# Value tiles in two buffers, loaded two tiles ahead, with joined PSUM banks for scores and values

## The chip, the cores and the metric

The kernel runs on one core of one Trainium2 chip. A core has TensorE (PE in the rows; PEld is its weight load), VectorE (DVE), ScalarE (ACT), GpSimd (POOL) and SyncE (SP), which here issues every DMA. Each engine takes its instructions in the order in which they stand in its queue and waits on semaphores for the others. The metric is the device time of one execution in microseconds.

## The reference

Attention over chunks, then two feed-forward layers, all in float32:

```python
# attention: batch 4, heads 8, sequence 768, head size 64, 8 memory slots
for c in range(nc):                     # chunks of 32 queries
    l_start = max(0, c * 32 - 16)
    r_end = min(S, c * 32 + 32 + 8)
    k_full = np.concatenate([mem_k, k[:, :, l_start:r_end]], axis=2)
    v_full = np.concatenate([mem_v, v[:, :, l_start:r_end]], axis=2)
    scores = scale * np.matmul(q_c, k_full.transpose(0, 1, 3, 2))
    a = np.exp(scores - np.max(scores, axis=-1, keepdims=True))
    a = a / (np.sum(a, axis=-1, keepdims=True) + 1e-09)
    out[:, :, c * 32:c * 32 + 32] = np.matmul(a, v_full)
...
x = out as 3072 tokens of 512           # 4 x 768 tokens, 8 heads x 64
h = x @ w_in;  x = (h * tanh(softplus(h))) @ w_out            # 512 -> 2048 -> 512
xn = x / rms(x) * rms_g
out = (silu(xn @ w_gate) * (xn @ w_val)) @ w_out2             # 512 -> 1536 -> 512
```

## The kernel before

The 3072 tokens are 24 tiles of 128 (`TSUB`), six to a batch (`SPB`). Three tiles make a block of 384 tokens, two blocks a pair (`TPP` = 6 tiles), and there are four pairs. Attention makes a pair's tokens; the first feed-forward product of that pair then runs beside the attention of the next pair.

Attention of a tile is five steps on TensorE, each with a step behind it on the other engines: `a` transposes queries and keys (L349, L306), `b` multiplies them into scores, 64 small matmuls over two PSUM banks (L371), `c` transposes the exponentials (L404), `d` multiplies them with the values, again 64 matmuls over two banks (L422), `e` transposes the result (L450). `b1` takes the maximum (L385) and subtracts it (L386) bank by bank and takes the exponential; `d1` divides by the sum (L436 to L440), also bank by bank. The steps of successive tiles are staggered by `att_list`: in one round stand `e` of tile t-4, `d` of t-3, `c` of t-2, `b` of t-1 and `a` of t. All of them take PSUM banks from `bank()`, which rotates through three.

Keys, queries and values come by `load_k`, `load_q`, `load_v`. The values go to one buffer, `vw`: two halves of eight heads, four overlapping chunks each, so eight DMAs a tile, with two more for the memory slots in the first tile of a batch. `mem_v_copy` then copies the memory values to the other three chunks on VectorE (L296), two copies a batch. A tile's values are loaded once the value product of the tile before has been issued.

The products are computed by a scheme with seven products of half size in place of eight. Six matmuls (L526 to L528, twice) are one product, seven products one group (`group`, `group1`), and a group has four banks X, Y, Z, V. X, Y and Z take a second product each, so a bank's first result must be read before the second is added, and its last result before the next group writes it. The reads are L537, L545 and L589 on ScalarE and L541, L553, L556 and L558 on VectorE. `group_banks(5)` hands the banks out in turn from five. Before a pair's first group, its tokens are added up (L502, L503 on VectorE, L504, L505 on GpSimd) and split into a high and a low part (`split`, L136 on ScalarE, L137 on VectorE) for seven operands `T`. The first of these needs the first block alone, the others both.

The weights are loaded raw (L132), converted (`cv_all`, L166 to L219) and kept or stored. The conversions are spread over the stages in small steps (`cv_upto`).

The order on each engine is not that of the code: a scheduler places the instructions by its own estimate of when each is ready. So an edit of banks, buffers or loads moves instructions on all engines.

## Time and profile before

| what | us |
|---|---|
| median of three runs | 1248.97 (1245.0 to 1252.62) |
| the profiled execution | 1247.89, of which its span 1246.1 |
| TensorE busy in the span | 1189.9 |
| VectorE busy | 858.1 |
| ScalarE busy | 623.7 |
| GpSimd busy | 289.0 |
| fill: attention of the first pair | 0 to 82 |
| first product beside attention, three stages | 82 to 181.5, 268.7, 358.5 |
| first product without attention | 358.5 to 422.4 |
| the rest | 422.4 to 1246 |

The profile is one execution. A matmul's busy time holds its way through the array, so successive matmuls overlap, and a busy TensorE is not one at its peak; the distance between starts tells the pace. The granted clock of TensorE is told as a share of full speed: 1.00 is 2.4 GHz, 0.50 is 1.2 GHz.

### The profile page before, as it was taken

What the parts mean: (1) busy time and instruction counts of PE and PEld (TensorE: products, weight loads), DVE (VectorE), ACT (ScalarE), POOL (GpSimd) and SP (SyncE); (2) the same over time, 40 slices, a digit from 0 to 9 for tenths busy, and PEclk for the clock granted to TensorE, in tenths of its full rate; (3) what the DMA queues carried; (4) which work ended last, traced back from release to release, by engine and by line L of the source; (5) the groups of instructions that cost most, each with busy time, mean ns of one, the idle gap of its engine ahead of it and who ended that gap; (6) DMA issues with size and microseconds to landing.
All of it is one profiled execution on the core that took longest, in us unless ns stands there. A gap on an engine that the chain in (4) does not pass through costs nothing.

```text
span 1246.1 us, 24931 instructions
## 1 busy us (share of the span) xinstructions
PE 1189.9 (95%) x9896; PEld 1144.8 (92%) x9896; DVE 858.1 (69%) x1418; ACT 623.7 (50%) x1050; POOL 289.0 (23%) x233
## 2 busy tenths in 40 slices
PE   5979899989979899999999999999999999999998
PEld 4768799979979899999999999999999999999998
DVE  4678794464476776768777587766667655898883
ACT  4455553343345687676867354443444432544442
POOL 1022130011033421113131221212122211433332
PEclk6579999999989899999999999999999999999999
DMA  8559779858439785575839779969476759644450
GB/s 190 127 168 295 210 225 306 268 145 261 146 129 368 250 274 167 200 259 187 301 101 387 308 263 402 342 246 363 170 288 258 294 203 348 184 136 136 138 150 34
DMA packets 213684, 287.43 MB, mean 231 GB/s; under 512 B 103232, under 2 KB 176960, under 8 KB 209344
## 3 DMA queue, kind: packets, MB, share of 16 engines
q1 hardware_dynamic: 213568, 285.85, 68.5%
q8 instruction: 77, 1.26, 0.4%
q14 instruction: 39, 0.32, 0.1%
HBM read 180.42 MB, written 105.38 MB: 229 GB/s over the span
## 4 chain that ended last, share of the span: by engine, by line
PE 82%; DVE 7%; DMA 7%; ACT 2%; issue 2%; SPq 1%; DVEq 0%; ACTq 0%
PE bk L526 13%; PE bk L527 13%; PE bk L528 13%; PE bk L610 7%; PE bk L611 7%; PE bk L609 7%; PE bk L724 5%; PE bk L722 5%; PE bk L723 5%; DMA T<-nt_scratch 3%; PE bk L422 2%; PE bk L371 2%; DVE T L137 1%; PE bk L306 1%; PE bk L404 1%
## 5 line engine op out<-in xcount | busy, mean ns | idle before, releaser
L526 PE MATMUL bk<-T,w 128*128 128x384 f32 x1120 | 384.6, 346 | 16.9 <-DVE g L558 6.8
L527 PE MATMUL bk<-T,w 128*128 128x384 f32 x1120 | 381.7, 341 | 0.8 <-DVE T L137 0.8
L528 PE MATMUL bk<-T,w 128*128 128x384 f32 x1120 | 375.5, 341 | 0.0
L526 PEld LDWEIGHTS bk<-T,w 128*128 128x128 f32 x1120 | 214.1, 191 | 23.8 <-DVE g L558 7.4
L527 PEld LDWEIGHTS bk<-T,w 128*128 128x128 f32 x1120 | 214.2, 191 | 2.4 <-DVE T L137 1.7
L528 PEld LDWEIGHTS bk<-T,w 128*128 128x128 f32 x1120 | 213.6, 191 | 0.6 <-DVE w L137 0.4
L610 PE MATMUL bk<-T,w 128*128 128x384 f32 x512 | 173.9, 340 | 0.2 <-DVE T L137 0.2
L609 PE MATMUL bk<-T,w 128*128 128x384 f32 x512 | 171.1, 338 | 2.8 <-ACT T L136 2.7
L611 PE MATMUL bk<-T,w 128*128 128x384 f32 x512 | 173.0, 338 | 0.0
L722 PE MATMUL bk<-w,T 128*128 128x256 f32 x504 | 143.2, 284 | 0.8 <-ACT T L136 0.8
L724 PE MATMUL bk<-w,T 128*128 128x256 f32 x504 | 142.9, 284 | 0.6 <-DVE T L137 0.6
L723 PE MATMUL bk<-w,T 128*128 128x256 f32 x504 | 142.6, 283 | 0.0
L553 DVE TENSOR_TENSOR s<-bk,s 128x384 f32<-128x384 f32 (+1 forms) x92 | 49.3, 536 | 85.1 <-PE bk L528 72.8
L609 PEld LDWEIGHTS bk<-T,w 128*128 128x128 f32 x512 | 96.5, 189 | 4.1 <-ACT T L136 3.0
L610 PEld LDWEIGHTS bk<-T,w 128*128 128x128 f32 x512 | 96.9, 189 | 1.2 <-DVE T L137 0.6
L722 PEld LDWEIGHTS bk<-w,T 128*128 128x128 f32 x504 | 96.5, 191 | 1.3 <-ACT T L136 1.3
L611 PEld LDWEIGHTS bk<-T,w 128*128 128x128 f32 x512 | 96.9, 189 | 0.8
L724 PEld LDWEIGHTS bk<-w,T 128*128 128x128 f32 x504 | 96.4, 191 | 0.8 <-DVE T L137 0.8
L723 PEld LDWEIGHTS bk<-w,T 128*128 128x128 f32 x504 | 96.8, 192 | 0.0
L557 POOL TENSOR_TENSOR v<-s,z 128x384 f32<-128x384 f32 x48 | 51.8, 1079 | 179.2 <-DVE s L553 123.8
L537 ACT COPY s<-bk 128x384 f32<-128x384 f32 (+1 forms) x92 | 42.8, 465 | 82.2 <-PE bk L528 69.7
L137 DVE TENSOR_TENSOR T<-w,T 128x768 fp32r<-128x768 f32 x60 | 74.9, 1259 | 12.1 <-ACT T L136 12.1
(123 smaller groups left out, 1904.9 us busy)
## 6 DMA issues: line engine op xcount, KB each, us to landing
T<-nt_scratch SPq DMA_DIRECT2D x49, 768.0 KB
g_scratch<-g SPq DMA_DIRECT2D x64, 384.0 KB
g<-g_scratch SPq DMA_DIRECT2D x64, 384.0 KB
h_scratch<-s SPq DMA_DIRECT2D x48, 384.0 KB
w<-h_scratch SPq DMA_DIRECT2D x24, 768.0 KB
w<-wi SPq DMA_DIRECT2D x9, 1792.0 KB
nt_scratch<-T SPq DMA_DIRECT2D x21, 768.0 KB
raw<-in_moe_w_out_dram SPq DMA_DIRECT2D x28, 512.0 KB
```

The source lines that it names most:

```text
L137: (eng or nc.vector).tensor_tensor(lo, src, hi.bitcast(F32), op=ALU.subtract)
L526: nc.tensor.matmul(ps, whi, xh, start=first and kk == 0, stop=False, **more)
L527: nc.tensor.matmul(ps, whi, xl, start=False, stop=False, **more)
L528: nc.tensor.matmul(ps, wlo, xh, start=False, stop=kk == 1, **more)
L553: nc.vector.tensor_tensor(u3, y, s1, op=ALU.add)
L557: nc.gpsimd.tensor_tensor(c22, u3, z5, op=ALU.add)
L609: nc.tensor.matmul(ps, ahi, bhi, start=start, stop=False)
L610: nc.tensor.matmul(ps, ahi, blo, start=False, stop=False)
L611: nc.tensor.matmul(ps, alo, bhi, start=False, stop=stop)
L722: nc.tensor.matmul(ps, t[:, 0, f], w[:, 0], start=first and f == 0, stop=False, **more)
L723: nc.tensor.matmul(ps, t[:, 0, f], w[:, 1], start=False, stop=False, **more)
L724: nc.tensor.matmul(ps, t[:, 1, f], w[:, 0], start=False, stop=f == HG - 1, **more)
```

## The change

Values get two buffers, in turn by tile, and a tile's values are loaded behind the value product two tiles before it. With two buffers the first two tiles of a batch load the memory values and copy them, and the copies move from VectorE to GpSimd. In the fill, the values of the first two tiles, the raw weights and the RMS gains are no longer loaded ahead of everything: `load_v(0)` comes ahead of the third piece of the list, the raw weights ahead of the fifth, `load_v(1)` ahead of the seventh, the gains behind the fill, and the conversions begin four pieces later.

Two PSUM banks become one tile of two banks, `bkp`, which scores and values use in turn. Transposes rotate through two banks of their own, and a group of products through four. `b1` and `d1` then work on both banks with one instruction each where they took two, and `p`, `pT` and `x` have one buffer each in place of two.

```diff
-    bk = [psp.tile([128, 512], F32, name=f"bk{c}") for c in range(8)]
+    bk = [psp.tile([128, 512], F32, name=f"bk{c}") for c in range(6)]
+    bk2 = psp.tile([128, 2, 512], F32, name="bkp")
+    bk += [bk2[:, e, :] for e in range(2)]
...
-    vw = atp.tile([128, NP, 4, D + 1], F32, tag="vw", name="vw")
+    vw = [atp.tile([128, NP, 4, D + 1], F32, tag=f"vw{u}", name="vw") for u in range(2)]
...
     def bank():
-        rot[0] = (rot[0] + 1) % 3
-        return bk[5 + rot[0]]
+        rot[0] = (rot[0] + 1) % 2
+        return bk[4 + rot[0]]
...
-        vt = vw
+        vt = vw[t % 2]
...
-            if i == 0:
+            if i < 2:
                 src = mem_v[b].rearrange("(a e) s d -> e s a d", e=2)[h2]
...
-        if t % SPB == 0:
+        if t % SPB < 2:
+            vt = vn[t]
             for p0 in (0, 64):
-                nc.vector.tensor_copy(
-                    vw[p0:p0 + NMEM, :, 0:3, :],
-                    vw[p0:p0 + NMEM, :, 3:4, :].to_broadcast([NMEM, NP, 3, D + 1]),
+                nc.gpsimd.tensor_copy(
+                    vt[p0:p0 + NMEM, :, 0:3, :],
+                    vt[p0:p0 + NMEM, :, 3:4, :].to_broadcast([NMEM, NP, 3, D + 1]),
...
-        ps = bank(), bank()
-        ps = [x[:, 0:256].rearrange("p (a k) -> p a k", a=NP) for x in ps]
+        ps = bk2[:, :, 0:256].rearrange("p e (a k) -> p e a k", a=NP)
...
-        mx = at2.tile([128, NP, 2], F32, tag="mx", name="mx")
-        p = at2.tile([128, NP, 2, 64], F32, tag="p", name="p")
-        for e in range(2):
-            nc.vector.reduce_max(mx[:, :, e], ps[e], axis=AX.X)
-            nc.vector.tensor_tensor(
-                p[:, :, e, :], ps[e],
-                mx[:, :, e].unsqueeze(2).to_broadcast([128, NP, 64]), op=ALU.subtract
-            )
+        mx = at2.tile([128, 2, NP], F32, tag="mx", name="mx")
+        p = at1.tile([128, NP, 2, 64], F32, tag="p", name="p")
+        nc.vector.reduce_max(mx, ps, axis=AX.X)
+        nc.vector.tensor_tensor(
+            p.rearrange("p a e k -> p e a k"), ps,
+            mx.unsqueeze(3).to_broadcast([128, 2, NP, 64]), op=ALU.subtract
+        )
...
-        if t + 1 < TSUB:
-            load_v(t + 1)
+        if t + 2 < TSUB:
+            load_v(t + 2)
...
-        for e in range(2):
-            nc.vector.tensor_scalar_add(sm[:, e, :], px[e][:, :, D], EPS_SUM)
+        nc.vector.tensor_scalar_add(sm, px[:, :, :, D], EPS_SUM)
...
-        banks = group_banks(5)
+        banks = group_banks(4)
...
-    load_v(0)
-    cv_prefetch(0)
-    nc.sync.dma_start(out=rmsg, in_=rms_g.rearrange("(c p) -> p c", p=128))
 
     first = att_list(0)
     for n, piece in enumerate(first):
+        if n == 2:
+            load_v(0)
+        if n == 6:
+            load_v(1)
+        if n == 4:
+            cv_prefetch(0)
         for fn, t in piece:
             fn(t)
-        cv_upto(CV_START * (n + 1) // len(first))
+        if n >= 4:
+            cv_upto(CV_START * (n + 1 - 4) // (len(first) - 4))
+    nc.sync.dma_start(out=rmsg, in_=rms_g.rearrange("(c p) -> p c", p=128))
```

How the order on the engines moves is shown at three places. The first is the DMA queue of SP at the start, behind the first key and query tiles. Before:

```order
L270 DMA qn<-in_q_dram 128x8x64
L282 DMA vw<-in_mem_v_dram 8x4x64
L291 DMA vw<-in_v_dram 40x4x64
L291 DMA vw<-in_v_dram 56x4x64 x3
L282 DMA vw<-in_mem_v_dram 8x4x64
L291 DMA vw<-in_v_dram 40x4x64
L291 DMA vw<-in_v_dram 56x4x64 x3
L132 DMA raw<-in_moe_w_in_dram 128x4x256 x2
L764 DMA rmsg<-in_moe_rms_g_dram 128x4x1
L260 DMA kn<-in_k_dram 128x8x64 x2
```

And now (L285, L294 are the value loads, L263 the key loads, L273 the query loads):

```order
L273 DMA qn<-in_q_dram 128x8x64
L285 DMA vw<-in_mem_v_dram 8x4x64
L294 DMA vw<-in_v_dram 40x4x64
L294 DMA vw<-in_v_dram 56x4x64 x2
L263 DMA kn<-in_k_dram 128x8x64
L294 DMA vw<-in_v_dram 56x4x64
L285 DMA vw<-in_mem_v_dram 8x4x64
L273 DMA qn<-in_q_dram 128x8x64
L294 DMA vw<-in_v_dram 40x4x64
```

The third key tile moved ahead of six value loads, the raw weights and the gains.

The second place is TensorE around the last transposes of attention, in the third stage. `T_...` is an operand of a pair and `w_...` the weights of a group; `T_4599` and `T_4619` belong to the fourth pair. Before:

```order
L450 MATMUL bk6_88<-ident_90,x_4569 128x128 x4
L526 MATMUL bk0_82<-T_4599,w_3829 128x384
L527 MATMUL bk0_82<-T_4599,w_3829 128x384
L528 MATMUL bk0_82<-T_4599,w_3829 128x384
L526 MATMUL bk0_82<-T_4599,w_3829 128x384
L527 MATMUL bk0_82<-T_4599,w_3829 128x384
L528 MATMUL bk0_82<-T_4599,w_3829 128x384
L526 MATMUL bk3_85<-T_4632,w_4004 128x384
L526 MATMUL bk2_84<-T_4619,w_4004 128x384
```

Now, first behind the last transposes (`T_3382` belongs to the third pair):

```order
L449 MATMUL bk4_86<-ident_89,x_4495 128x128 x4
L525 MATMUL bk0_82<-T_3382,w_3951 128x384
L526 MATMUL bk0_82<-T_3382,w_3951 128x384
L527 MATMUL bk0_82<-T_3382,w_3951 128x384
L525 MATMUL bk0_82<-T_3382,w_3951 128x384
L526 MATMUL bk0_82<-T_3382,w_3951 128x384
```

and 42 matmuls later, where the fourth pair's operands `T_4524` and `T_4544` begin:

```order
L527 MATMUL bk2_84<-T_3454,w_3951 128x384
L525 MATMUL bk0_82<-T_4524,w_3951 128x384
L526 MATMUL bk0_82<-T_4524,w_3951 128x384
L527 MATMUL bk0_82<-T_4524,w_3951 128x384
L525 MATMUL bk0_82<-T_4524,w_3951 128x384
L526 MATMUL bk0_82<-T_4524,w_3951 128x384
L527 MATMUL bk0_82<-T_4524,w_3951 128x384
L525 MATMUL bk1_83<-T_4544,w_3951 128x384
```

Before, a product of the fourth pair's first operand follows the last transposes, and then those that need its sums. Now all seven products of the third pair's last group stand between.

The third place is VectorE at the same border: the sums of the fourth pair, its splits and the reads of the groups' banks. Before:

```order
L502 TENSOR_TENSOR xb<-xb 128x768
L172 SCALAR_TENSOR_TENSOR ca<-raw,ca 128x512
L503 TENSOR_TENSOR t<-xb 128x768
L178 ISA ca<-ca,lr 128x1024
L556 TENSOR_TENSOR g<-bk_86,u_4628 128x384
L558 SCALAR_TENSOR_TENSOR g<-bk_82,s_4617 128x384
L137 TENSOR_TENSOR T<-t,T 128x768
L137 TENSOR_TENSOR T<-xb,T 128x768
L137 TENSOR_TENSOR T<-t,T 128x768
```

Now:

```order
L501 TENSOR_TENSOR xb<-xb 128x768
L502 TENSOR_TENSOR t<-xb 128x768
L540 TENSOR_TENSOR u_4553<-bk_83,s_4542 128x384
L139 TENSOR_TENSOR T<-t,T 128x768
L139 TENSOR_TENSOR T<-xb,T 128x768
L552 TENSOR_TENSOR s_4542<-bk_83,s_4542 128x384
L139 TENSOR_TENSOR T<-t,T 128x768
L555 TENSOR_TENSOR g<-bk_84,u_4553 128x384
L557 SCALAR_TENSOR_TENSOR g<-bk_85,s_4542 128x384
L139 TENSOR_TENSOR T<-xb,T 128x768 x3
```

The conversions no longer stand between the sums, and the reads of the third pair's last group now stand between the splits.

## Rows read from the trace of the kernel before

**Rows 1.** Windows by stage: from:to, sum, then busy PE, PEld, DVE, ACT, POOL, PEclk, DMA

```profile
0.00:82.00 82.00, 57.90 (x965) 43.79 (x966) 47.23 (x115) 37.22 (x62) 9.47 (x15) 0.63 0.67 158
82.00:181.50 99.50, 94.38 (x1215) 85.23 (x1215) 87.17 (x182) 59.74 (x109) 24.57 (x22) 0.94 0.81 239
181.50:268.70 87.20, 82.62 (x1186) 75.11 (x1185) 42.76 (x111) 29.79 (x54) 10.23 (x9) 0.99 0.81 247
268.70:358.50 89.80, 83.09 (x1124) 76.76 (x1123) 45.66 (x109) 32.86 (x60) 12.77 (x11) 0.98 0.59 180
358.50:422.40 63.90, 60.54 (x331) 59.18 (x331) 47.12 (x72) 35.53 (x66) 24.56 (x20) 0.95 0.76 280
422.40:1246.00 823.60, 811.37 (x5080) 804.72 (x5080) 588.16 (x835) 428.58 (x703) 207.43 (x158) 0.99 0.67 237
```

**Rows 2.** Timeline in the fourth stage: start, duration, engine, line, operation, count

```profile
384.79 0.51 PE L528 MATMUL bk<-T,w 128*128 128x384 f32 x2
...
385.14 0.33 PE L526 MATMUL bk<-T,w 128*128 128x384 f32 x1
...
386.91 0.55 DVE L556 TENSOR_TENSOR g<-bk,u 128x384 f32<-128x384 f32 x1
```

**Rows 3.** Waits of TensorE over the span: total, times, longest

```profile
PE bk L526 <- DVE g L558: 6.8, 1, 6.8
```

**Rows 4.** Timeline of SP's DMA queue at the start

```profile
4.31 1.09 SPq L282 DMA_DIRECT2D vw<-in_mem_v_dram  x1
5.45 1.63 SPq L291 DMA_DIRECT2D vw<-in_v_dram  x4
...
11.31 2.40 SPq L260 DMA_DIRECT2D kn<-in_k_dram  x2
```

**Rows 5.** Timeline of TensorE in the fill; in brackets idle before, and releaser

```profile
17.74 1.12 PE L306 MATMUL bk<-ident,kn 128*128 128x128 f32 x4 [3.31 <-DMA kn<-in_k_dram]
...
27.59 1.54 PE L371 MATMUL bk<-kw,qT 64*32 64x64 f32 x64 [0.92 <-DVE x L440]
...
60.02 1.08 PE L422 MATMUL bk<-vw,pT 64*32 64x65 f32 x64 [0.26 <-DVE p L386]
...
63.63 2.80 PE L422 MATMUL bk<-vw,pT 64*32 64x65 f32 x60 [0.25 <-DMA vw<-in_v_dram]
69.39 1.11 PE L306 MATMUL bk<-ident,kn 128*128 128x128 f32 x4 [2.96 <-DVE x L440]
```

**Rows 6.** Timeline of VectorE at the end of the fill

```profile
68.21 0.56 DVE L296 COPY vw<-vw 8x780 f32<-8x780 f32 x1 [1.51 <-DMA vw<-in_mem_v_dram]
```

**Rows 7.** Timeline of TensorE at the border of the second and third stage

```profile
264.88 0.79 PE L371 MATMUL bk<-kw,qT 64*32 64x64 f32 x52 [1.01 <-DVE kw L315]
...
267.48 0.98 PE L349 MATMUL bk<-ident,qn 128*128 128x128 f32 x4 [1.81 <-DVE kw L320]
```

**Rows 8.** Timeline of VectorE at the border of the third and fourth stage

```profile
354.47 2.56 DVE L503 TENSOR_TENSOR t<-xb 128x768 f32<-128x768 f32 x1
...
357.55 0.55 DVE L556 TENSOR_TENSOR g<-bk,u 128x384 f32<-128x384 f32 x1
358.02 0.54 DVE L558 SCALAR_TENSOR_TENSOR g<-bk,s 128x384 f32<-128x384 f32 x1
```

**Rows 9.** Windows, columns as in rows 1: the border after the third stage, the fill

```profile
351.50:364.00 12.50, 5.68 (x22) 5.44 (x21) 11.43 (x12) 6.90 (x11) 6.02 (x3) 0.73 0.29 105
10.00:60.00 50.00, 39.15 (x664) 29.98 (x661) 31.00 (x80) 23.89 (x42) 3.21 (x4) 0.52 0.70 168
```

**Rows 10.** Groups by line: busy, mean ns, idle before

```profile
L386 DVE TENSOR_TENSOR p<-bk,mx 128x256 f32<-128x256 f32 x48 | 18.8, 415 | 0.2
...
L557 POOL TENSOR_TENSOR g<-s,z 128x384 f32<-128x384 f32 x32 | 36.6, 1145 | 165.8 <-DVE s L553 110.3 <-issue 24.2 <-DMA vw<-in_v_dram 9.9
```

**Rows 11.** Timeline of VectorE in the second stage

```profile
247.23 0.56 DVE L556 TENSOR_TENSOR g<-bk,u 128x384 f32<-128x384 f32 x1 [0.48 <-PE bk L528]
```

**Rows 12.** One line's instructions, L503: duration minimum, median, maximum in ns

```profile
L503 DVE TENSOR_TENSOR t<-xb x4: 953/2518/2557, 73.8 to 354.5; 128x768 f32<-128x768 f32 x4
```

26 lines of the change are left out of this document (13 added, 13 removed).

## Prediction

> **What bounds the kernel now.** I read the busy time of the engines by stage first [rows 1]. The stages are the fill (attention of the first two token blocks, 0 to 82 us), three stages that each put one pair's first feed-forward product beside the next pair's attention (82 to 181.5, 181.5 to 268.7, 268.7 to 358.5), a fourth without attention (to 422.4), and the rest. The rest is 811.37 of 823.60 us TensorE, and the change gives it no instruction to add, remove or resize, so what can be won lies in the first 422 us. A product of a group is six matmuls; a start every 0.175 us (two from 384.79, the next at 385.14) [rows 2] makes 1.05 us, a group of seven products 7.35 us, eight groups 58.8 us. The second and third stages take 87.2 and 89.8 us, the fourth 63.9.
>
> Then I looked at what TensorE waits for: the longest wait behind the first load is one of 6.8 us for a VectorE read [rows 3]. The timeline puts it and the others at three places: the fill [rows 4 to 6], the border of the second and third stage [rows 7] and that of the third and fourth [rows 8]. Around the last one the granted clock is 0.73 of full, and in the fill 0.52, so nearly all matmuls there run at 1.2 GHz [rows 9]. VectorE is busy 87.17 of 99.50 us in the first stage, 42.76 and 45.66 in the next two [rows 1].
>
> **The change part by part**, against the profiled execution: 1247.89 us, of which the span is 1246.1, 1.8 us lies around it. The median of the runs is 1.1 us above; I take the sum off the median.
>
> *First loads.* The third key tile is issued at 11.31 us, behind ten value DMAs, two weight loads and the gains [rows 4]; it lands 6.4 us later, at 17.7, and TensorE waits 3.31 us for it [rows 5]. In the new order one memory and three value DMAs stand ahead of it: 4.31 + 1.09 + 3 x 0.41 = 6.6 us. With the same 6.4 us it lands at 13.0, 4.7 us earlier, more than the wait. I take 3 off; bounds 0 (the queue is full anyway) and 5 (later tiles move up as well). The conversions start four pieces later and hide behind what is left of the fill: the group that needs the first weight is among its last work.
>
> *Two value buffers and the memory copies.* At the end of the fill the last value product takes 2.80 us for 60 matmuls where 64 took 1.08 (63.63 and 60.02 us) [rows 5], since the one buffer is loaded only after the value product before it: 1.8 us. Then VectorE, in order, stands before a copy of the next batch's memory values and waits 1.51 us for their DMA, copies 0.56, and only then divides [rows 6]; the next transposes wait 2.96 us for that [rows 5]. Loaded two tiles ahead and copied on GpSimd, both fall away, together 4.8 us. Late next is the division itself (some 1 us after the product) on the one joined pair, so I take 4; bounds 0 and 5. GpSimd's copies are not in the trace. By the nearest rows one lies between VectorE's 0.56 us [rows 6] and 780 elements at GpSimd's two-input pace, 780 x 1145/384 ns = 2.3 us [rows 10]; I take 2.3, the row of its own engine. The two of the first tile then take 4.6 us beside that tile's scores, softmax and transposes, which hide them; without that cover they would cost up to 4.6 us.
>
> *Joined banks in the fill.* Scores and values now take turns on one pair, transposes on two banks. A value product must wait for the scores' subtraction, and the scores for the division; both held before too, since three banks rotated through eight uses a step. But a transpose no longer has to wait for the use just before it. Five waits of the kind of 0.92 us at 27.59 [rows 5] stand between 25 and 48 us; they can go or stay: 0, bounds -4 and +4. Most of the fill is TensorE at half clock, busy 39.15 of 50 us at 0.52 [rows 9]. The fill together: -7, bounds -14 and +4.
>
> *The border of the third and fourth stage.* Before, the order leaves nothing of the third stage behind the last transposes: what follows is one product of the next pair, done ahead, and products that need its sums. So TensorE waits while VectorE does 2.56 us of sum and, last, two evacuations, to 358.56 us [rows 8]. In the new order all seven products of the third stage's last group stand behind the last transposes: 7.35 us. The chain there, with 2.56 us for its longest part and three operations of under a microsecond each, is some 5 us, and the second product of the next stage starts 8.4 us after the transposes. The 6.8 us wait goes, and with it most of what the half clock there takes: 0.27 of 12.5 us, 3.4 us [rows 9], of which a third falls on the wait itself. Late next are the evacuations that stand between the splits in VectorE's order (three splits of 1 to 1.6 us ahead of the read of the third bank): some 2 us. So -8; bounds -10 and -3. *The border before it* [rows 7] has waits of 1.01 and 1.81 us, with 1.4 more in two others; there too a group's 42 matmuls now stand behind the last transposes. I take -5 (4.3 and the clock, less a short wait), bounds -7 and 0.
>
> *Fewer VectorE instructions.* 256 elements take 415 ns [rows 10], 384 take 0.55 us [rows 2], so 512 cost about 0.69 us against 0.83 for two: 0.14 us for each of reduction, subtraction, division and, as an estimate, the small sum, 0.57 us a tile, 3.4 us a stage; and eight copies of 0.56 us leave. In the second and third stage VectorE is half idle, so this is worth nothing; in the first, where it is busy 88% and TensorE waits, I take 3 of the 3.4.
>
> *Four banks for a group, not five.* A bank must be read two products after its last write (2.1 us), not three. In the second and third stage VectorE mostly waits for the product and reads at once, as at 247.23 us [rows 11], and nothing would wait. In the fourth it works on conversions too: there the read of a third bank begins at 386.91 and ends at 387.46, some 2.2 us after the product's last matmul ended at 385.30 [rows 2]. Such reads, and the sums at the borders, would make TensorE wait 0.2 to 1.7 us a group: +2.5 for the fourth stage, bounds 0 and 6. In the first stage attention lies between the products and stretches the time: +2, bounds 0 and 8. No row shows a four-bank rotation; the lower end is no wait at all, and I stay near it because reads like that at 247.23 us are nearer to most groups.
>
> Sum: -7 - 8 - 5 - 3 + 2.5 + 2 = **-18.5 us**, 1230.5.
>
> *What speaks against GpSimd's copies.* The same sum on VectorE (line 503) takes 953 ns at best and 2518 ns at the median of its four uses at the borders, where GpSimd works on the same tiles [rows 12]: 1.57 us more. A copy that lies beside a split or a sum may do the same; eight copies at the two later borders, at 1.57 us each, would be 12.6 us of VectorE, which rival B takes up. The Trainium skill ("SBUF — State Buffer", Who interferes with whom) says that a VectorE instruction with two SBUF inputs contends with a GpSimd instruction that reads SBUF, and that the one issued second waits for the whole of the first; the trace agrees for the sum, no row shows a copy, and by this rule the forecast's sum would lose up to those 12.6 us.
>
> **The rivals.**
>
> *A, slower: four banks make TensorE wait in every group.* If VectorE or ScalarE is one product late in each of the 32 groups, that is 33.6 us, against the 23 us that the other terms give: +10.6, 1259.5. It decides from 0.7 us a group on. For it: the read 2.2 us late in the fourth stage, and VectorE at 88% in the first. Against it: half of the groups lie in stages with an idle VectorE. The Trainium skill ("TensorE: Matmul & The Clock Gate", A second HAM failure mode) tells of a kernel in which cycling through PSUM banks made short idles and dropped the clock again and again; that would add to this price, and no row here shows it for five banks.
>
> *B, about the same: GpSimd's copies hold up the borders.* GpSimd is in order; four copies stand ahead of its two sums at the end of the fill, others near the next two borders. If each set of four (9.2 us) comes late by half, for want of its value DMA or by blocking VectorE, 4.6 us at three borders is 13.8: 1244. For it: VectorE did stand 1.51 us before such a copy. Against it: the loads are issued a tile earlier, and the fourth and seventh product need those sums last.
>
> *C, the fill doesn't shrink:* the loads only change places, and TensorE at half clock or the DMA queue (0.70 busy between 10 and 60 us) sets its length [rows 9]. Then the 7 us stay: 1237.5.
>
> **How the numbers follow.** Forecast 0.60, A 0.10, B 0.14, C 0.16. About 0.5% (6.2 us) is what a measurement of this kernel can tell from no change. The forecast's own terms reach from 1216 (bounds of fill and borders together) to 1243; with C and B inside, 1217 to 1250 holds 8 in 10. Faster: the forecast but for its upper edge, nearly all of C, and a few parts of B's upper side: 0.76. Within 0.5%: most of B, the edges of the forecast and of A: 0.15. Slower: A, with a little for borders that a new order places badly: 0.09.
>
> **What would show it.** First loads: the third key tile issued near 7 us and no wait of TensorE for keys between 14 and 18 us. Buffers: no VectorE wait for the memory values, the last value product of the fill in about 1 us, first full run of groups 5 to 9 us earlier than at 82 us. Borders: no wait over 2 us at the start of the fourth stage, the clock near full there, the third stage near 82 us. Banks: in the fourth stage waits of TensorE for the evacuations (lines 552 to 557 of the changed kernel) of 2 to 3 us in all; over 10 us would prove A. Joining: one subtraction of about 0.69 us in place of two of 0.415. I would be wrong if the fill stays at 82 us, if the first stage grows past 100 us, or if a wait for GpSimd's copies shows on TensorE.

## The result, and the profile after

The changed kernel takes 1227.39 us (median of 4 runs, 1225.22 to 1233.01) against 1249.36 us before (1245.0 to 1252.62): a ratio of 0.984, 95% interval 0.982 to 0.987. Run a second time beside three experiments it took 1230.25 us against 1244.4, a ratio of 0.988 (0.986 to 0.989). The forecast was 1230.5. The changed kernel is 22.0 us faster in the first session and 14.2 in the second, where 18.5 were forecast. The total is right, but partly by chance: the experiments show a gain and a loss in the first stage that the forecast did not have and that nearly cancel, and a fill that got shorter in another way than it said.

The profiled execution is the slowest of its four: span 1231.2 us, 14.9 less than the 1246.1 of before. The windows by stage of the changed kernel, columns as in [rows 1] (each stage here begins with the second product of its first group; on that measure the stages of the kernel before begin at 77.6, 176.5, 270.5 and 360.7 us, and the rest at 422.4):

```profile
0.00:71.50 71.50, 44.84 (x958) 33.41 (x959) 40.06 (x83) 34.80 (x59) 16.34 (x25) 0.76 0.81 170
71.50:171.80 100.30, 89.21 (x1202) 78.78 (x1201) 86.05 (x157) 57.24 (x107) 27.76 (x26) 0.95 0.93 255
174.10:262.90 88.80, 85.84 (x1124) 78.38 (x1124) 44.20 (x82) 30.04 (x55) 16.71 (x14) 0.96 0.80 238
262.90:344.40 81.50, 81.47 (x1179) 75.00 (x1179) 44.03 (x84) 34.31 (x61) 13.25 (x10) 1.00 0.60 185
344.40:406.60 62.20, 58.63 (x332) 57.00 (x331) 45.03 (x71) 34.33 (x64) 23.10 (x19) 1.00 0.80 295
406.60:1231.00 824.40, 809.62 (x5080) 802.41 (x5080) 586.00 (x838) 427.22 (x705) 214.64 (x159) 1.00 0.67 237
```

TensorE is busy 81.47 of 81.50 us in the third stage, at a granted clock of 1.00, where before it was idle for 6.8 of 90.2 us, the one wait of [rows 3]. The first stage is the odd one: 100.3 us to the end of its last product, where the kernel before took 97.1 on the same measure, and TensorE is idle for 11 of them.

From start to start, each stage and its difference to before, in the profiled executions: fill 71.5 us (-6.1), first stage 102.5 (+3.6), second 88.9 (-5.1), third 81.4 (-8.8), fourth 62.2 (+0.5), the rest 824.7 (+1.0). Sum -14.9.

The early loads. SP's queue and TensorE's timeline of the changed kernel (start, duration, engine, line, operation, count, idle before and releaser in brackets), to be held against [rows 4] and [rows 5]:

```profile
6.67 0.39 SPq L263 DMA_DIRECT2D kn<-in_k_dram  x1
...
11.30 1.08 PE L310 MATMUL bk<-ident,kn 128*128 128x128 f32 x4 [0.25 <-DMA kn<-in_k_dram]
...
60.72 1.19 PE L423 MATMUL bkp<-vw,pT 64*32 64x65 f32 x64
```

The third key tile is issued at 6.67 us (the forecast said 6.6), used at 11.30 after a wait of 0.25 us, and the last value product of the fill takes 1.19 us instead of 2.80. All three are as forecast. But the waits of the fill have not gone: TensorE's idle time in it is 26.7 of 71.5 us, and 23.7 of 77.6 in the kernel before. What fell is its busy time, from 53.93 to 44.84 us for about as many matmuls (the first row of the windows above; this is the row of before):

```profile
0.00:77.60 77.60, 53.93 (x949) 40.72 (x949) 42.83 (x109) 32.82 (x55) 8.25 (x15) 0.64 0.69 160
```

The border of the third and fourth stage, window from the last transposes to 12.5 us later, against the 0.73 of [rows 9]:

```profile
335.90:348.40 12.50, 12.48 (x73) 11.98 (x72) 11.99 (x14) 7.97 (x13) 7.19 (x4) 1.00 0.32 124
```

TensorE is busy 12.48 of 12.50 us; the wait of 6.8 us [rows 3] has gone. The waits of TensorE in the whole fourth stage, with the handover at its end (us in total, times, longest):

```profile
PE bk L525 <- ACT z L544: 1.4, 2, 0.9
PE bk L525 <- DVE g L555: 1.1, 1, 1.1
PE bk L608 <- DVE s L552: 1.1, 1, 1.1
```

Joined operations and GpSimd's copies, from the groups by line (busy, mean ns, idle before):

```profile
L300 POOL COPY vw<-vw 8x780 f32<-8x780 f32 x16 | 16.8, 1049 | 51.4 <-DMA vw<-in_mem_v_dram 50.5 <-PE bk L527 0.8
L388 DVE TENSOR_TENSOR p<-bkp,mx 128x512 f32<-128x512 f32 x24 | 16.5, 688 | 0.6
```

One subtraction takes 688 ns, as worked out from two sizes. A copy on GpSimd takes 1.05 us (at best 0.83), not the 2.3 taken.

### The profile page after: what moved, and what is told of

Same layout as the page of the kernel before. It is cut to its first block, busy times and chain, and to the rows that moved or that the text cites. A ratio compares the mean times of both kernels' runs of the same rounds, so it can differ in the third digit from the quotient of the medians.

```text
span 1231.2 us, 24871 instructions
## 1 busy us (share of the span) xinstructions
PE 1171.6 (95%) x9896; PEld 1126.5 (91%) x9896; DVE 847.3 (69%) x1314; ACT 620.2 (50%) x1050; POOL 311.8 (25%) x251
## 4 chain that ended last, share of the span: by engine, by line
PE 62%; DMA 8%; DVE 7%; ACT 4%; issue 2%; POOL 2%; SPq 0%; DVEq 0%; ACTq 0%; POOLq 0%
PE bk L525 10%; PE bk L526 9%; PE bk L527 9%; PE bk L721 4%; PE bk L722 4%; PE bk L723 4%; DMA T<-nt_scratch 4%; PE bk L609 2%; PE bk L610 2%; PE bk L608 2%; DMA g<-g_scratch 2%; DVE T L139 2%; PE bkp L610 1%; PE bkp L609 1%; PE bkp L608 1%
## 5 line engine op out<-in xcount | busy, mean ns | idle before, releaser
L525 PE MATMUL bk<-T,w 128*128 128x384 f32 x976 | 339.9, 350 | 13.3 <-DMA T<-nt_scratch 3.9
L526 PE MATMUL bk<-T,w 128*128 128x384 f32 x976 | 331.6, 340 | 1.9 <-DVE T L139 1.9
L527 PE MATMUL bk<-T,w 128*128 128x384 f32 x976 | 328.8, 339 | 1.7 <-DVE w L139 1.6
L525 PEld LDWEIGHTS bk<-T,w 128*128 128x128 f32 x976 | 185.8, 191 | 23.9 <-DMA T<-nt_scratch 5.3
L526 PEld LDWEIGHTS bk<-T,w 128*128 128x128 f32 x976 | 185.8, 190 | 3.5 <-DVE T L139 2.9
L527 PEld LDWEIGHTS bk<-T,w 128*128 128x128 f32 x976 | 185.3, 190 | 2.5 <-DVE w L139 2.5
L608 PE MATMUL bk<-T,w 128*128 128x384 f32 x384 | 128.9, 339 | 1.1 <-DVE s L552 1.1
L609 PE MATMUL bk<-T,w 128*128 128x384 f32 x384 | 129.8, 338 | 0.0
L610 PE MATMUL bk<-T,w 128*128 128x384 f32 x384 | 129.0, 336 | 0.0
L721 PE MATMUL bk<-w,T 128*128 128x256 f32 x396 | 111.6, 282 | 0.0
L723 PE MATMUL bk<-w,T 128*128 128x256 f32 x396 | 111.5, 282 | 0.0
L722 PE MATMUL bk<-w,T 128*128 128x256 f32 x396 | 111.3, 281 | 0.0
L139 DVE TENSOR_TENSOR T<-w,T 128x768 fp32r<-128x768 f32 x60 | 77.4, 1301 | 11.4 <-ACT T L138 11.4
L722 PEld LDWEIGHTS bk<-w,T 128*128 128x128 f32 x396 | 75.4, 190 | 0.0
L556 POOL TENSOR_TENSOR g<-s,z 128x384 f32<-128x384 f32 x32 | 34.4, 1075 | 161.6 <-DVE s L552 85.2
L721 PEld LDWEIGHTS bk<-w,T 128*128 128x128 f32 x396 | 75.1, 190 | 0.0
L723 PEld LDWEIGHTS bk<-w,T 128*128 128x128 f32 x396 | 75.1, 190 | 0.0
L608 PEld LDWEIGHTS bk<-T,w 128*128 128x128 f32 x384 | 72.2, 188 | 1.9 <-ACT w L138 1.4
L609 PEld LDWEIGHTS bk<-T,w 128*128 128x128 f32 x384 | 72.3, 188 | 1.1 <-DVE T L139 0.3
```

What stands on the lines that cost most here:

```text
L139: (eng or nc.vector).tensor_tensor(lo, src, hi.bitcast(F32), op=ALU.subtract)
L525: nc.tensor.matmul(ps, whi, xh, start=first and kk == 0, stop=False, **more)
L526: nc.tensor.matmul(ps, whi, xl, start=False, stop=False, **more)
L527: nc.tensor.matmul(ps, wlo, xh, start=False, stop=kk == 1, **more)
L556: nc.gpsimd.tensor_tensor(c22, u3, z5, op=ALU.add)
L608: nc.tensor.matmul(ps, ahi, bhi, start=start, stop=False)
```

## The experiments

The change has three parts: the order of the first loads, the two buffers with GpSimd's copies, and the regrouped banks with the joined operations. Each was run alone, each was left out, so all eight combinations are known; four more runs follow one open place. Each time is given as a ratio to the kernel before, measured in the same session.

### Each part alone

First loads alone:

```diff
-    load_v(0)
-    cv_prefetch(0)
-    nc.sync.dma_start(out=rmsg, ...)
     for n, piece in enumerate(first):
+        if n == 2:
+            load_v(0)
+        if n == 4:
+            cv_prefetch(0)
...
-        cv_upto(CV_START * (n + 1) // len(first))
+        if n >= 4:
+            cv_upto(CV_START * (n + 1 - 4) // (len(first) - 4))
+    nc.sync.dma_start(out=rmsg, ...)
```

> The kernel before with only the first loads put in order of need (values before the third piece, conversions from the fifth, gains last), one value buffer, eight separate banks. The forecast's theory: the third key tile is issued near 7 us, TensorE's wait for it goes, the fill ends about 3 us earlier than at 77.6 us (second product of stage 1), the borders stay as they were: 3 us faster than the kernel before, about 1246. Rival C (loads only change places, the half clock or the DMA queue sets the length of the fill): fill end within 1 us of 77.6, time within 1 us of the kernel before. If the whole 6.1 us that the fill of the changed kernel gained come from the loads: 6 us faster.

Measured: 1249.38 us, ratio 1.000 (0.998 to 1.002). The key tile moved as forecast and the fill ended 6.7 us earlier, at 70.9, twice the forecast's 3. But nothing of it is left at the end: the first stage takes 102.2 us from start to start (98.9 before), the rest 826.9 (823.7). A shorter fill is worth nothing where the later stages give it back.

Two buffers alone:

```diff
-    vw = atp.tile([128, NP, 4, D + 1], F32, tag="vw", name="vw")
+    vw = [atp.tile([128, NP, 4, D + 1], F32, tag=f"vw{u}", name="vw") for u in range(2)]
...
-                nc.vector.tensor_copy(
+                nc.gpsimd.tensor_copy(
...
-        if t + 1 < TSUB:
-            load_v(t + 1)
+        if t + 2 < TSUB:
+            load_v(t + 2)
```

The diff is cut: `p`, `pT` and `x` have one buffer each in this part, as in the changed kernel, and keep two in the banks alone. No run separates this from the second value buffer, and "buffers" below means both, with the copies on GpSimd.

> The kernel before with only the two value buffers, filled two tiles ahead, memory copies on GpSimd, one buffer each for p, pT and x; old order of first loads (the second tile's values before the seventh piece), eight separate banks, five for a group. The forecast's theory: the last value product takes about 1.1 us instead of 2.8 and VectorE's wait for memory values goes, fill end 4 us earlier, borders as before, 4 us faster than before. Rival B (copies on GpSimd hold up the sums at the borders): stage 1 grows by 3 us or more here, as it did in the changed kernel (97.1 to 100.3 us), and the net is 0 to 1 us or slower. If instead the growth of stage 1 in the changed kernel comes from the banks, stage 1 is 97 us or less here.

Measured: 1246.79 us, ratio 0.9986 (0.997 to 1.0004). The fill is 5.7 us shorter, the second stage 4.3, the third 2.7 longer, the rest 9.7 longer. The first stage did not grow (98.4 us), so the copies on GpSimd alone don't lengthen it.

Banks alone (four for a group, a joined pair, two for transposes; joined operations):

```diff
-    bk = [psp.tile([128, 512], F32, name=f"bk{c}") for c in range(8)]
+    bk = [psp.tile([128, 512], F32, name=f"bk{c}") for c in range(6)]
+    bk2 = psp.tile([128, 2, 512], F32, name="bkp")
+    bk += [bk2[:, e, :] for e in range(2)]
...
-        banks = group_banks(5)
+        banks = group_banks(4)
```

> The kernel before with only the banks regrouped: four for a group, two joined for scores and values, two for transposes, joined VectorE instructions; one value buffer, old first loads. The forecast's theory: the two borders give 13 us less whatever part of the new order stands here (five products of the third stage's last group stand behind its last transposes), joined instructions 2 to 3, four banks cost 4.5: 11 us faster than before (bounds 4 to 16), fill end within 4 us of 77.6. If the growth of stage 1 comes from four banks, stage 1 is 100 us or more here; if from the copies on GpSimd, 96 us or less. Rival A (four banks make TensorE wait in every group): slower than before.

Measured: 1246.89 us, ratio 0.998 (0.996 to 1.0003); 11 us were forecast. The fill is 4.3 us shorter, the first stage 3.0, the third 3.7; the second is 4.6 longer and the fourth 3.0 longer.

Four banks for a group, and nothing else:

```diff
-        banks = group_banks(5)
+        banks = group_banks(4)
```

> The kernel before with one number changed: a group takes four banks in turn instead of five; attention keeps its three banks, one bank lies idle in the first four stages. The forecast's theory: waits for evacuations cost 4.5 us (2 in stage 1, 2.5 in stage 4); two products of the third stage's last group now stand behind its last transposes where none did, which gives back some 2 to 3 us there: 0 to 3 us slower than before. Rival A: 0.7 us or more a group, 20 us slower or more. If the four banks are themselves what makes the borders better: 5 us or more faster than before, with the wait of 6.8 us at the start of stage 4 gone.

Measured: 1256.19 us, ratio 1.0057 (1.003 to 1.008), 8 us slower; 0 to 3 were forecast. It is not rival A, which has a wait in every group: TensorE's long waits behind 400 us stand at two handovers (from the last product of one stage to the first of the next), where the kernel before waits 2.2 and 2.7 us:

```profile
PE bk L526 <- ACT s L602: 5.1, 1, 5.1
PE bk L609 <- ACT g L589: 4.9, 1, 4.9
```

In the groups between 77 and 400 us the waits for evacuations are 1.2 us in all. The second is the handover of the fourth stage to the rest. The first lies at 718 us, in the rest, where groups take eight banks in turn in both kernels; the kernel with the first loads alone has a wait as long at that place (5.10 us, shown below) and is not slower. The wait of 6.8 us at the start of the fourth stage is 3.1 us here. So what the 8 us are made of is open but for the 2.2 us at the fourth stage's end.

Its window in the fill must be read with care, against the second row of [rows 9]:

```profile
10.00:60.00 50.00, 38.24 (x658) 28.75 (x657) 30.89 (x80) 24.30 (x42) 3.20 (x4) 1.00 0.73 168
```

The 1.00 is no measured clock: this profile has no clock record ahead of 84.1 us. The one product in the window starts a matmul every 0.32 us:

```profile
54.81 0.52 PE L528 MATMUL bk<-T,w 128*128 128x384 f32 x1
55.13 0.52 PE L526 MATMUL bk<-T,w 128*128 128x384 f32 x1
55.45 0.52 PE L527 MATMUL bk<-T,w 128*128 128x384 f32 x1
```

That is the pace of the kernel before from 358.6 to 363 us, where its granted clock is 0.50 (starts at 360.06 and 360.38), and not the 0.175 us of [rows 2]. So this fill ran as slowly as the one before, and its length (77.3 against 77.6 us) says nothing of what the half clock costs. In the same way the windows of the other fills count the time ahead of the first record (8.2 us in the kernel before, 16.1 in the changed one) as 1.00, so their clocks are compared below from 16.1 us on.

### Two parts together

Buffers and banks, the first loads of the changed kernel put back:

```diff
+    load_v(0)
+    cv_prefetch(0)
+    nc.sync.dma_start(out=rmsg, ...)
     for n, piece in enumerate(first):
-        if n == 2:
-            load_v(0)
         if n == 6:
             load_v(1)
-        if n == 4:
-            cv_prefetch(0)
...
-        if n >= 4:
-            cv_upto(CV_START * (n + 1 - 4) // (len(first) - 4))
-    nc.sync.dma_start(out=rmsg, ...)
+        cv_upto(CV_START * (n + 1) // len(first))
```

> The changed kernel with the first loads in the old order (values of the first tile, weights and gains ahead of the third key tile; second tile's values before the seventh piece). Theory 'together': the borders are won by the two buffers and the four-bank groups jointly, the loads only shift the fill, and what they win in the fill goes into a longer first stage (conversions start later): within 4 us of the changed kernel, about 1229; stage 1 near 98 us and the fill near 74 to 77 us. Theory 'sum of parts' (my forecast): 3 us slower than the changed kernel, stage 1 unchanged at 100 us. Rival 'all three are needed': as slow as the parts alone, about 1246.

Measured: 1218.21 us, ratio 0.979 (0.978 to 0.981). This is 12 us faster than the changed kernel in the same session (1230.25).

Loads and banks, with one buffer:

```diff
-        vt = vw[t % 2]
+        vt = vw
...
-                nc.gpsimd.tensor_copy(
+                nc.vector.tensor_copy(
...
-        if t + 2 < TSUB:
-            load_v(t + 2)
+        if t + 1 < TSUB:
+            load_v(t + 1)
```

> The changed kernel with one value buffer, filled one tile ahead, memory copies on VectorE, two buffers each for p, pT and x; new first loads and joined banks stay. Theory 'together': without the second buffer the last transposes of a stage stand no earlier against the products; at the border of the second and third stage only two products of the old pair stand behind the last transposes of that batch's first half, and the gain is gone there: 1242 to 1247, with the border of second and third stage about 10 us longer than in the changed kernel. Theory 'sum of parts': 4 us slower than the changed kernel, 1231.

Measured: 1238.31 us, ratio 0.996 (0.994 to 0.997), some 8 us over the changed kernel in the same session (1230.25): beside the other parts the buffers are worth twice the 4 us that they were given.

Loads and buffers, with the banks as before:

```diff
-    bk = [psp.tile([128, 512], F32, name=f"bk{c}") for c in range(6)]
-    bk2 = psp.tile([128, 2, 512], F32, name="bkp")
-    bk += [bk2[:, e, :] for e in range(2)]
+    bk = [psp.tile([128, 512], F32, name=f"bk{c}") for c in range(8)]
...
-        banks = group_banks(4)
+        banks = group_banks(5)
```

> The changed kernel with eight separate banks, five in turn for a group, three for attention, and VectorE instructions by halves; new first loads and two buffers stay. Theory 'together': with five banks products of two groups interleave at the borders and TensorE waits for the new pair's sums at the start of stage 4 as in the kernel before (over 5 us): 1242 to 1248. Theory 'sum of parts': 13 us of the borders and the 3 of VectorE are lost, 4.5 of the bank waits come back: 1239. If the loads and buffers alone made the gain: 1230.

Measured: 1241.67 us, ratio 0.998 (0.996 to 0.999): without the banks nearly all of the gain is gone too.

All three, the changed kernel again, with no edit:

> The changed kernel itself once more, for a second profile and a narrower interval beside the three above: 1225 to 1230, fill end near 71.5 us, stage 1 near 100 us if the longer first stage belongs to the kernel, 97 us or less if it was that one execution.

Measured: 1230.25 us, ratio 0.988 (0.986 to 0.989). Its stages agree with the first profile within 1.1 us (fill 70.6, first stage 103.6, then 89.0, 81.4, 62.5), so the long first stage belongs to the kernel.

All eight together, in us of the profiled execution from stage start to stage start, and the ratio to the kernel before:

| parts | fill | first | second | third | fourth | rest | ratio |
|---|---|---|---|---|---|---|---|
| none | 77.6 | 98.9 | 94.0 | 90.2 | 61.7 | 823.7 | 1 |
| loads | 70.9 | 102.2 | 94.5 | 91.2 | 61.9 | 826.9 | 1.000 |
| buffers | 71.9 | 98.4 | 89.7 | 92.9 | 60.9 | 833.4 | 0.999 |
| banks | 73.3 | 95.9 | 98.6 | 86.5 | 64.7 | 825.6 | 0.998 |
| loads, buffers | 69.6 | 97.2 | 91.6 | 91.4 | 60.8 | 828.2 | 0.998 |
| loads, banks | 71.6 | 92.4 | 98.0 | 85.3 | 64.1 | 824.7 | 0.996 |
| buffers, banks | 71.6 | 92.1 | 86.8 | 81.9 | 61.9 | 820.7 | 0.979 |
| all three | 71.5 | 102.5 | 88.9 | 81.4 | 62.2 | 824.7 | 0.984, 0.988 |

Two things stand out. Any part alone shortens the fill by 4 to 7 us, and a second part adds little (together 6 to 8). And buffers and banks win 0.1% and 0.2% alone, 2.1% together: the second and third stage are short only where both are there.

Why both are needed is seen in the stretch from the last transposes of a stage's attention to the second product of the next stage. The windows of the whole stretch at the border of the second and third stage and at that of the third and fourth (columns as in [rows 1]). Before:

```profile
261.80:270.50 8.70, 5.46 (x86) 4.38 (x85) 8.03 (x16) 5.56 (x10) 4.96 (x3) 0.84 0.67 147
351.50:360.70 9.20, 2.38 (x9) 2.14 (x8) 8.13 (x9) 5.10 (x9) 5.72 (x3) 0.77 0.27 94
```

Buffers alone, and its one wait of TensorE at the later border:

```profile
253.90:260.00 6.10, 4.13 (x89) 3.72 (x87) 5.13 (x9) 4.74 (x8) 4.12 (x4) 1.00 0.68 162
344.30:352.90 8.60, 2.94 (x13) 2.62 (x12) 7.55 (x8) 4.40 (x8) 5.65 (x3) 0.79 0.22 66
```

```profile
PE bk L528 <- DVE g L560: 5.7, 1, 5.7
```

Banks alone:

```profile
259.70:267.80 8.10, 5.05 (x80) 3.51 (x78) 7.26 (x9) 3.78 (x7) 4.14 (x3) 0.50 0.71 141
347.90:354.30 6.40, 6.40 (x40) 6.40 (x39) 5.06 (x6) 3.01 (x5) 4.42 (x2) 1.00 0.20 79
```

Buffers and banks:

```profile
239.90:250.50 10.60, 10.60 (x73) 9.84 (x71) 8.31 (x15) 5.25 (x10) 9.09 (x7) 1.00 0.74 188
323.90:332.40 8.50, 8.50 (x51) 8.32 (x50) 8.00 (x9) 4.80 (x8) 5.73 (x3) 1.00 0.24 93
```

The stretch itself hardly shrinks, 6 to 11 us in all four: sums, splits and evacuations take their time. What differs is the third number, TensorE's busy time in it. With both parts it works all the time, mostly on products that stand behind the last transposes; with five banks (buffers alone) the later border has 13 matmuls and the old wait; with banks alone that border is mended (6.40 of 6.40 us) and the earlier is not. There the timeline of TensorE shows the last value product of the stage, with the one buffer:

```profile
253.72 0.68 PE L421 MATMUL bkp<-vw,pT 64*32 64x65 f32 x4
254.55 0.30 PE L421 MATMUL bkp<-vw,pT 64*32 64x65 f32 x2 [0.16 <-DMA vw<-in_v_dram]
255.00 0.30 PE L421 MATMUL bkp<-vw,pT 64*32 64x65 f32 x2 [0.15 <-DMA vw<-in_v_dram]
...
256.62 1.13 PE L421 MATMUL bkp<-vw,pT 64*32 64x65 f32 x52 [0.25 <-DMA vw<-in_v_dram]
```

It goes piece by piece, as the loads land, and the stage's own products ended at 250.9 us: nothing is left to run beside it. The second buffer lets the attention finish ahead of the products (last transposes at 239.9 us, last product at 248.5); the four banks keep a group's products together, so that they stand there whole. Each without the other leaves one border open. Where the copies of the memory values run plays no part in this: with both parts and the copies on VectorE (two runs below) the third stage takes 81.7 us too.

### Why the new first loads cost some 10 us beside the other two parts

The loss is in the first stage, 102.5 against 92.1 us. The changed kernel's VectorE, then GpSimd, then TensorE, at the end of that stage:

```profile
161.65 3.55 DVE L139 TENSOR_TENSOR w<-sm,w 128x512 fp32r<-128x512 f32 x2
165.12 2.59 DVE L139 TENSOR_TENSOR T<-t,T 128x768 fp32r<-128x768 f32 x1
...
169.82 0.55 DVE L540 TENSOR_TENSOR u<-bk,s 128x384 f32<-128x384 f32 x1
```

```profile
160.91 1.51 POOL L300 COPY vw<-vw 8x780 f32<-8x780 f32 x1 [0.54 <-DMA vw<-in_mem_v_dram]
162.50 2.15 POOL L504 TENSOR_TENSOR xb<-xb 128x768 f32<-128x768 f32 x1
164.61 2.29 POOL L503 TENSOR_TENSOR t<-t,xb 128x768 f32<-128x768 f32 x1
```

```profile
163.02 0.44 PE L527 MATMUL bk<-T,w 128*128 128x384 f32 x1 [0.40 <-DVE w L139]
165.25 0.44 PE L527 MATMUL bk<-T,w 128*128 128x384 f32 x1 [1.16 <-DVE w L139]
170.43 0.45 PE L525 MATMUL bk<-T,w 128*128 128x384 f32 x1 [2.60 <-DVE u L540]
```

The last two splits of the stage's last weight (line 139, w from sm) stand behind both of VectorE's sums, TensorE waits for them, and the first read of that group (line 540) stands behind two more splits and a softmax. And the splits lie beside GpSimd's copy and sums: the two of the first row end at 165.2 after GpSimd's sum ends at 164.65, the split of 768 elements at 167.71 after 166.90. In the kernel with the old loads both splits are done before VectorE's second sum, at 156.18, and before GpSimd's sums begin, at 159.76:

```profile
154.97 1.28 DVE L139 TENSOR_TENSOR w<-sm,w 128x512 fp32r<-128x512 f32 x2
...
157.25 0.54 DVE L540 TENSOR_TENSOR u<-bk,s 128x384 f32<-128x384 f32 x1
```

Four suspects: the late start of the conversions, GpSimd's copies, the loads themselves (raw weights that land late), and the place of those splits.

Conversions and gains started as before, values still by need:

```diff
+    cv_prefetch(0)
+    nc.sync.dma_start(out=rmsg, ...)
...
-        if n == 4:
-            cv_prefetch(0)
...
-        if n >= 4:
-            cv_upto(CV_START * (n + 1 - 4) // (len(first) - 4))
+        cv_upto(CV_START * (n + 1) // len(first))
```

> The changed kernel with the weight conversions (first loads of weights, gains and the pieces that convert) started as in the kernel before, while the value loads keep the new order. Theory 'conversions start late': the 9 to 12 us that the old first loads win come from the conversions, so stage 1 is near 92 us and the time near 1218. Theory 'border order and GpSimd': the order at the border of first and second stage is that of the changed kernel (both splits of the last weight behind the sums' second instruction), so stage 1 stays near 100 us: 1226 to 1230.

Measured: 1229.42 us, ratio 0.986 (0.983 to 0.989), the same as the changed kernel; its profiled execution, 9 us over the median of its runs, has a first stage of 110.2 us. The start of the conversions is not the cause, and the order at the border is the changed kernel's: the two splits take 3.55 us there too, from 167.70.

Copies back on VectorE:

```diff
-                nc.gpsimd.tensor_copy(
+                nc.vector.tensor_copy(
```

> The changed kernel with one edit: the copies of the memory values go back to VectorE (both buffers, new first loads and joined banks stay). In its order at the border of the first and second stage one of the last weight's two splits stands ahead of the sums and the first read of the stage's last group ahead of the sum splits, as in the kernel with the old first loads; in the changed kernel both stand behind. Theory 'border order and GpSimd': stage 1 gets shorter by 6 to 10 us (near 92 us instead of 100 to 102), the two splits take about 0.7 us each instead of 2.3, 1218 to 1222. Theory 'conversions start late': stage 1 stays at 100 us or grows, since VectorE gets eight to sixteen copies of 0.56 us more: 1228 to 1233. My forecast (copies hidden on GpSimd): 2 to 5 us slower than the changed kernel.

Measured: 1223.73 us, ratio 0.982 (0.979 to 0.984); the first stage takes 94.1 us. The forecast's reasoning would have it slower, and it is 3 to 7 us faster. One split stands ahead of VectorE's first sum (158.00), the other ahead of its second (162.17):

```profile
156.49 0.68 DVE L139 TENSOR_TENSOR w<-sm,w 128x512 fp32r<-128x512 f32 x1
...
158.87 0.67 DVE L139 TENSOR_TENSOR w<-sm,w 128x512 fp32r<-128x512 f32 x1
...
159.74 1.93 DVE L300 COPY vw<-vw 8x780 f32<-8x780 f32 x1
161.70 0.56 DVE L540 TENSOR_TENSOR u<-bk,s 128x384 f32<-128x384 f32 x1
```

The old first loads and the copies on VectorE together, the first diff of the section on two parts and this one:

```diff
-                nc.gpsimd.tensor_copy(
+                nc.vector.tensor_copy(
```

> The kernel that joins the old first loads and copies of the memory values on VectorE with the two buffers and the regrouped banks. Theory 'border order and GpSimd': both edits mend the same place, so they don't add: 1215 to 1221, as with either alone. If they add, 1208 to 1212. If the copies on VectorE cost it what they take (0.56 us each in a stage that VectorE fills): 1221 to 1225.

Measured: 1225.14 us, ratio 0.982 (0.980 to 0.985), first stage 95.6 us. They don't add: with the old loads the copies are better on GpSimd (0.979), with the new ones on VectorE. So where the copies run does not decide by itself.

One number in the changed kernel, the end to which the conversion pieces of the first stage are spread:

```diff
-    bt = slots((att_list(1), 56), (0, 98), tail_of(1),
+    bt = slots((att_list(1), 56), (0, 106), tail_of(1),
```

> The changed kernel with one number changed: the pieces of the first stage's weight conversions are spread over the stage to an end of 106 instead of 98 (the same pieces, still capped at the same last one, each a little earlier). In its order both splits of the last weight, and all of the last group's evacuations, stand ahead of the first pair of sum splits on VectorE; the first loads stay new and the copies stay on GpSimd. Theory 'border order': what the new first loads cost in the changed kernel comes from the place of those splits, so stage 1 takes 91 to 95 us instead of 100 to 102, each split about 0.7 us instead of 1.8 to 2.3, and the time is 1216 to 1222, with new loads. Theory 'the loads themselves cost it' (raw weights land late, whatever the order): the earlier pieces wait for their data, stage 1 stays at 99 us or more, 1226 or more.

Measured: 1217.86 us, ratio 0.976 (0.975 to 0.978), the lowest of all (the old loads' interval, 0.978 to 0.981, just touches it), with the new loads and GpSimd's copies. The first stage takes some 91 us, and the splits are done before either sum (159.54 and 161.14):

```profile
153.17 1.28 DVE L139 TENSOR_TENSOR w<-sm,w 128x512 fp32r<-128x512 f32 x2
...
156.34 0.55 DVE L540 TENSOR_TENSOR u<-bk,s 128x384 f32<-128x384 f32 x1
```

Among the kernels with buffers and banks, where both splits stand ahead of VectorE's second sum the first stage is 91 to 96 us (old loads, copies on VectorE, both, the changed number); where they stand behind it, 102 to 110 (the changed kernel twice, conversions as before). This does not hold outside them: with the first loads alone both splits stand ahead of both sums (163.56 and 165.59, the sums at 167.46 and 168.94), and the first stage still takes 102.2 us. ScalarE's waits for raw weights, 12.6 and 11.4 us in the first stage of the changed kernel's two profiles, are 0.8 us with the old loads but still 8.4 us with the changed number: late raw weights alone don't decide.

How much is explained: TensorE is idle for 11.4 us in the first stage of the changed kernel, 3.8 with the old loads, which is 7.6 of their 10.4 us; about half of the 7.6 lies in the stage's last 22 us. The rows price 4.16 us of these waits there (0.40, 1.16 and 2.60), behind splits that took 3.9 us longer (3.55 - 1.28 and 2.59 - 0.95). The other half lies ahead of the border and was not taken apart. The last experiment isolates the place of the splits no better: it moves all conversions of the stage a little, and with them attention. Its first stage holds 1125 matmuls where the changed kernel's holds 1228, its second 1228 against 1124 at the same 88.9 us; 4.0 of its 11 us are less idle time (7.4 us). So that the place of the splits is part of the cause is likely; that it is the whole of it is not shown.

## Why the prediction was right, and where it was right by chance

*The borders of the second and third and of the third and fourth stage* (-5 and -8). Right in size: -5.1 and -8.8 us, and in mechanism: the full group behind the last transposes, the clock at 1.00, no wait of TensorE above 0.5 us at either border. What the forecast did not say is that this order needs both the second buffer and the four banks; it put the whole gain down to the order as it read it.

*The fill* (-7). Right in size (-6.1), wrong as a sum and in its mechanism. The loads were given 3 us and the buffers 4; alone they win 6.7 and 5.7, the banks 4.3, and all three together no more than one. The forecast took waits of TensorE off, but in the changed kernel's fill TensorE is idle for 26.7 us instead of 23.7. The waits that it named come back elsewhere: the third key tile costs 0.25 us at 11.30, but another costs 2.9 at 70.81; TensorE waits 4.9 us for the queries' evacuation, 1.9 for the softmax, and 4.0 at value products for nothing that the trace names. The gain is busy time, 9.1 us less for about as many matmuls, and it is so in all eight combinations: busy 42.9 to 50.2 us with any part, 53.9 before, idle 21.7 to 28.7. From 16.1 us on, where both profiles have clock records, the granted clock of the fill is 0.68 instead of 0.58, and at the higher clock the same matmuls are shorter (last section). That fits the gain; no run changes the clock alone, and the forecast had no term for it in the fill.

*First loads, the step that failed.* "The conversions start four pieces later and hide behind what is left of the fill": the delay at the start does no harm by itself, as the run with the old conversions shows, but the new first loads, beside the other two parts, put the last weight's splits behind the sums at the end of the first stage, and TensorE is idle there and in the groups before for 11.4 us instead of 3.8. Beside the other parts the edit costs 7 to 12 us (0.984 and 0.988 against 0.979; 12 by the medians of one session) where 3 were to be won.

*The border of the first and second stage* was not in the sum at all. The first stage was given -3 for VectorE's instructions and +2 for the banks, -1 in all; it took +3.6, and at 102.5 us it grew past the 100 that the prediction named as a sign of being wrong. With the old loads it changes by -6.8 us, with the changed number by some -7. So the forecast missed a gain of some 7 us there, of which it had 1 and which was not taken apart, and a loss of some 11; that the two nearly cancel in the total is luck.

*Four banks.* In the fourth stage +2.5 was forecast; its products end 61.1 us after its start instead of 59.0, +2.1, and the waits there are 2.5 us in all behind the evacuations. But the wait at the handover to the rest shrank from 2.7 to 1.1 us, so the stage costs +0.5 from start to start. The same edit alone costs 8 us, where the forecast's theory had 0 to 3; the handover of the fourth stage, at which the forecast did not look, is 2.2 of it (4.9 instead of 2.7), and the other part is open.

*Rivals.* A does not hold in the groups: 2.5 us of waits in the fourth stage where over 10 were to prove it. C does not hold as a forecast: the fill shrank. Its thought that the half clock sets the fill's length is not refuted; the shorter fills come with a higher clock and less busy time. B came true in part and at one border: GpSimd's copies wait for their memory values, its sums follow late, and VectorE's splits lie beside them; that is likely a part of what the first stage lost. Its price for a copy, 2.3 us, was more than twice too high (1.05).

*What the forecast left alone.* The rest was taken to stay at 823.6 us. It does in the changed kernel (+1.0), but in the eight combinations it runs from 820.7 to 833.4, though its instructions are the same: the order moves there too. One place, TensorE at the handover behind the second product stage, in the kernel with the first loads alone:

```profile
711.87 0.69 PE L526 MATMUL bk<-T,w 128*128 128x384 f32 x1 [5.10 <-ACT s L602]
```

Before, the wait at this place took 2.21 us. Single executions of one kernel differ by up to 12 us, so differences of 2 or 3 us in the rest of one profile may be chance; that of the buffers alone (+9.7) is not explained.

## What to carry to other kernels

Where a scheduler lays the order anew, the parts of a change don't add: two edits that win nothing alone can win 2% together, and a third that is right by its own place can take a third of it back at another border. So price every border that the new order touches, not only those with a wait today; the one that looked clean before was where a good part of the loss came. And when a stage gets shorter, compare busy and idle time before and after: here the fill got shorter while its idle time grew. A wait is mended when enough independent work stands behind its cause, and this can be read from a window: the matmuls between the last transposes and the next stage's products.

## What the runs showed of the hardware

*VectorE beside GpSimd.* A split of 512 elements takes 0.64 to 0.69 us alone, and the two of the pair at 161.65 take 1.32 and 2.31 us where GpSimd runs; a split of 768 elements 0.95 and 2.59 us. In the rows at 161.65 and 165.12 the pair and the single split end 0.55 and 0.81 us after the GpSimd instruction beside it, so they wait for that instruction and then run about their usual time. Operations of VectorE with their data in PSUM (lines 387, 388, 439) don't show it: 24 subtractions lie between 675 and 692 ns. The Trainium skill ("SBUF — State Buffer", Who interferes with whom) says that a VectorE instruction with two SBUF inputs contends with a GpSimd instruction that reads SBUF, and that whoever issues first holds the other up for the whole instruction; the rows above agree. It says the same of plain copies in their fast modes, and the copy of the memory values on VectorE agrees: 0.56 us as a rule, 1.93 us at 159.74, beside GpSimd's sum that began at 159.02 and took 2.23 us.

*The clock and the matmuls of attention.* In the changed kernel's fill the granted clock is 0.50 from 30 to 40 us and 1.00 from 40.0 to 46.8 us. 64 score matmuls take 1.18 us in the first stretch and 0.86 in the second, four transposes 1.06 and 0.60:

```profile
35.77 1.18 PE L374 MATMUL bkp<-kw,qT 64*32 64x64 f32 x64 [0.83 <-DVE x L439]
37.79 1.06 PE L449 MATMUL bk<-ident,x 128*128 128x128 f32 x4
40.61 0.60 PE L353 MATMUL bk<-ident,qn 128*128 128x128 f32 x4
41.37 0.86 PE L374 MATMUL bkp<-kw,qT 64*32 64x64 f32 x64 [0.16 <-DVE x L439]
```
